# In-place softmax features, three KV banks, a centred second layernorm, and reciprocals as a power on GpSimd

## The chip, the cores and the metric

The kernel runs on one core of a Trainium2 chip. The metric is the device time of one execution in microseconds; the first result is the median of two executions of each kernel, an experiment's that of four or six, and e2 and e6 ran once, for the profile. This core has no second die to compare with, so an execution counts as slow when it lies over 1.5% above the fastest of its kernel. Engines are named as the profile names them: PE (TensorE, matmuls), PEld (its weight loads), DVE (VectorE), ACT (ScalarE), POOL (GpSimd) and SP (DMA issue).

## The reference, cut to what matters

```python
def _A_ref(x, wqkv, w_phi, wo):            # S = 2048, D = 640, H = 32 heads of Dh = 20
    q, k, v = ...                          # x @ wqkv
    pq = einsum("bhsd,hdf->bhsf", q, w_phi);  pk = einsum("bhsd,hdf->bhsf", k, w_phi)
    phi_q = concat([softmax(pq), softmax(-pq)], -1)      # 64 softmaxes of 20 for each row
    phi_k = concat([softmax(pk), softmax(-pk)], -1)
    kv = einsum("bhsf,bhsd->bhfd", phi_k, v);  z = phi_k summed over s
    o = einsum("bhqf,bhfd->bhqd", phi_q, kv) / (einsum("bhqf,bhf->bhq", phi_q, z)[..., None] + 1e-6)
    return o.reshape(B, S, D) @ wo
def _B_ref(x, w_gate, w_up, w_down):       # F = 1536
    return ((x @ w_gate) * (x @ w_up)) @ w_down
h  = x + _A_ref(layernorm(x), ...)
h2 = h + _B_ref(layernorm(h), ...)
```

The rows are handled in 16 tiles of 128. All k tiles must be done before `kv` exists, and all of `kv` before the first numerator `phi_q @ kv`. So there are three stages: features and KV accumulation; a transition (numerators, normaliser, output projection, second layernorm, first FFN matmul); then four blocks of FFN, with the remaining q tiles made beside them.

## The kernel before

The program is written through a recorder. It gets a list of operations with **declared costs**, finds an order for each engine by list scheduling with these costs, and inserts semaphore waits wherever two operations touch the same **64-byte granule** of SBUF. The parts that matter:

```python
GRAN = 64
def _keys(self, ap):                  # which granules an operand touches
    ...
        b0, b1 = o * esz, (o + span) * esz - 1
        for g in range(b0 // gran, b1 // gran + 1):
            keys.add((name, g))
# resolve(): a write of a key waits for that key's last writer and readers; a read for its writer
...
def program(name):                    # each engine runs its list in order
    ...
        for o in op.deps:
            eng.wait_ge(*o.val)
        ins = op.fn(eng)
...
    e_p  = pool("e", sb("e_r", 3 * 2 * D), 0, 2 * D, 3)          # three buffers of exponentials
    sr_p = pool("sr", sb("sr", 3 * 4 * H, FP32), 0, 4 * H, 3)    # 128 floats each: sums, reciprocals
...
    def soft(ps, outs):
        ek = e_p.new()
        sr = sr_p.new()
        act(ek[:, 0:D], ps, ACT.Exp)
        act(ek[:, D:2 * D], ps, ACT.Exp, scale=-1.0)
        R.add("vector", lambda e: e.tensor_reduce(...), [ek], [sr[:, 0:2 * H]], cost=1.48)
        R.add("vector", lambda e: e.reciprocal(out=real(sr)[:, 2 * H:4 * H], in_=real(sr)[:, 0:2 * H]), ..., cost=0.56)
        for dst, esel, rsel in outs:                              # 2 (k) or 3 (q) multiplies
            tt("gpsimd", dst, esel(ek), rsel(rr), ALU.mult)
...
    acc = psum.new(2, starts=(6,))             # KV chunks 0 to 7, beside the projections
    acc2 = psum.new(1, starts=(7, 6))          # chunks 8 to 10: a second pass after the features
...
    def watt(t):                               # output projection, residual, second layernorm
        ...
        tt("vector", x_all[:, t, :], pr[:, 0:D], x_all[:, t, :], ALU.add)
        ln_stats(t)                            # two batch statistics and their aggregate, DVE
        ln_rs(t, 1)                            # Ln, Exp on ACT, one small DVE operation
        ln_apply(t, hT[:, b, :, P * q:P * (q + 1)])
```

The softmax here doesn't subtract the row's maximum and nothing guards it: scores larger than these inputs give would overflow.

## Time and profile before

| | |
|---|---|
| median | 337.76 us (337.29 to 338.23) |
| profiled span | 331.5 us (another execution, of 333.26 us) |
| busy: PE, DVE, ACT, POOL | 295.8, 184.9, 154.0, 89.9 us |
| first numerator matmul | 97.2 us |
| first FFN matmul | 136.0 us |

The windows view gives the busy time of each engine in a stretch, with the granted PE clock (PEclk). From 140 us on, PE is busy 9.8 us or more in every 10 us at clock 1.00, but for the last 11 us. The stretch ahead of that is where time is to be had:

```profile
core 0: us, PE busy (x) PEld busy (x) DVE busy (x) ACT busy (x) POOL busy (x), PEclk, DMA share, GB/s
70.00:80.00 10.00, 6.55 (x58) 4.07 (x58) 5.19 (x6) 4.99 (x8) 5.18 (x6) 1.00 0.00 1
90.00:100.00 10.00, 6.61 (x57) 5.38 (x57) 6.55 (x16) 4.04 (x9) 7.88 (x9) 0.83 0.72 173
100.00:110.00 10.00, 7.48 (x26) 3.17 (x27) 2.67 (x4) 6.82 (x14) 2.64 (x3) 0.68 0.90 177
120.00:130.00 10.00, 5.20 (x22) 1.94 (x20) 8.04 (x20) 9.05 (x22) 4.97 (x6) 0.88 0.60 115
```

The groups by form for the softmax features. After the count stand busy us and the mean ns of one, then the engine's idle time before them and what ended it:

```profile
L717 DVE TENSOR_REDUCE sr<-e_r 128x64 f32<-128x1280 bf16 x32 | 46.4, 1464 | 16.7 <-ACT e_r L590 16.7
L596 POOL TENSOR_TENSOR phq<-e_r,sr 128x600 bf16<-128x600 bf16 x32 | 37.8, 1202 | 111.3 <-DVE sr L720 98.3 <-DMA wkv<-phq 6.9 <-DVE mv L672 5.4
L596 POOL TENSOR_TENSOR r<-e_r,sr 128x1200 bf16<-128x1200 bf16 x16 | 35.5, 2227 | 27.5 <-DVE sr L720 27.5
L720 DVE RECIPROCAL sr<-sr 128x64 f32<-128x64 f32 x32 | 16.8, 537 | 0.3
```

The waits view (who waited for whom: us in total, times, longest). ACT's exponentials wait for POOL, as an e buffer is free only after POOL's multiply. DVE's reduces wait for ACT:

```profile
DVE sr L717 <- ACT e_r L590: 16.7, 10, 6.6
ACT e_r L590 <- POOL phq L596: 8.4, 5, 3.0
ACT e_r L590 <- POOL r L596: 4.6, 3, 3.5
```

And two lines of the timeline, in which a small DVE operation with two SBUF inputs, 0.15 us where no POOL instruction runs beside it, lasts almost as long as the POOL multiply beside it:

```profile
36.93 2.22 POOL L596 TENSOR_TENSOR r<-e_r,sr 128x1200 bf16<-128x1200 bf16 x1 [3.13 <-DVE sr L720]
37.18 1.99 DVE L672 SCALAR_TENSOR_TENSOR mv<-mv 128x2 f32<-128x2 f32 x1
```

### The profile page before, as it was taken

Reading aid. Unit: us, or ns where it says so; the run is one execution under the profiler, and the core shown is the slowest. Engines: PE = TensorE matmul, PEld = TensorE weight load, DVE = VectorE, ACT = ScalarE, POOL = GpSimd, SP = SyncE. Lnnn points to the kernel's source line nnn. Section 1 sums busy time; section 2 is a strip of 40 time slices with the busy share of each in tenths; the row PEclk is TensorE's granted clock in tenths of the full one; section 3 lists DMA queues with packets and bytes.
Section 4 is the critical chain, followed back from the end, with each engine's and each line's share of the span. In section 5 each row is a group of like instructions: output and inputs, shape, how many; then the busy total and the mean of one; then the engine's idle time right before and its main releaser. Section 6 shows DMA issues by size and latency. Waiting matters only on the chain.

```text
span 331.5 us, 4759 instructions
## 1 busy us (share of the span) xinstructions
PE 295.8 (89%) x1856; PEld 155.2 (47%) x1890; DVE 184.9 (56%) x328; ACT 154.0 (46%) x287; POOL 89.9 (27%) x104
## 2 busy tenths in 40 slices
PE   2988899859576894999999999999999999999996
PEld 2646666436262331444455444445543445544453
DVE  3898998726963586736541346955234583133331
ACT  4787797724638558621520675331048342022200
POOL 7147678685782036230000002303000000000000
PEclk9999999999977896899999999999999999999999
DMA  8567098930579236140301000541300013100011
GB/s 243 158 164 213 5 208 203 244 129 2 103 177 220 44 63 128 21 88 0 61 20 59 22 0 0 65 83 42 104 0 2 2 21 77 42 0 2 0 42 59
DMA packets 55466, 25.82 MB, mean 78 GB/s; under 512 B 45935, under 2 KB 54163, under 8 KB 55443
## 3 DMA queue, kind: packets, MB, share of 16 engines
q1 hardware_dynamic: 53299, 22.89, 30.8%
q10 hardware_dynamic: 2144, 2.62, 2.4%
q8 instruction: 15, 0.25, 0.3%
q14 instruction: 8, 0.07, 0.1%
HBM read 11.87 MB, written 2.62 MB: 44 GB/s over the span
## 4 chain that ended last, share of the span: by engine, by line
PE 71%; DVE 10%; ACT 9%; POOL 5%; issue 2%; DMA 2%; SPq 0%; POOLq 0%; ACTq 0%
PE ps L579 70%; DVE sr L717 4%; ACT e_r L590 3%; POOL r L596 3%; ACT xn L677 2%; DMA r<-in_A_wqkv_dram 2%; DVE st L664 1%; DVE mv L672 1%; ACT r L590 1%; PE ps L691 1%; DVE sr L720 1%; DVE r L596 1%; ACT lnd L590 1%; POOL phq L596 1%; POOL r L614 1%
## 5 line engine op out<-in xcount | busy, mean ns | idle before, releaser
L579 PE MATMUL ps<-xnT,wgu 128*128 128x512 bf16 x469 | 105.7, 379 | 1.2 <-issue 0.5
L590 ACT ACTIVATE r<-ps 128x512 bf16<-128x512 f32 (+3 forms) x88 | 53.0, 611 | 93.7 <-PE ps L579 93.4
L596 DVE TENSOR_TENSOR r<-ps,r 128x512 bf16<-128x512 f32 (+2 forms) x72 | 49.0, 689 | 75.5 <-PE ps L579 49.2
L579 PE MATMUL ps<-r 128*128 128x128 bf16 (+6 forms) x612 | 71.4, 274 | 4.5 <-DVE KV L802 3.8
L596 POOL TENSOR_TENSOR phq<-e_r,sr 128x600 bf16<-128x600 bf16 (+1 forms) x48 | 42.2, 910 | 111.3 <-DVE sr L720 98.3
L579 PEld LDWEIGHTS ps<-xnT,wgu 128*128 128x128 bf16 x480 | 45.8, 98 | 56.6 <-issue 2.4
L579 PEld LDWEIGHTS ps<-r 128*128 128x128 bf16 (+2 forms) x620 | 46.7, 113 | 29.6 <-DVE KV L802 4.2
L717 DVE TENSOR_REDUCE sr<-e_r 128x64 f32<-128x1280 bf16 x32 | 46.4, 1464 | 16.7 <-ACT e_r L590 16.7
L579 PE MATMUL ps<-wkv,xnT 128*128 128x128 bf16 (+1 forms) x310 | 45.3, 297 | 8.3 <-ACT e_r L590 4.8
L590 ACT ACTIVATE e_r<-ps 128x640 bf16<-128x640 f32 x64 | 41.8, 703 | 19.6 <-POOL phq L596 8.4
L596 POOL TENSOR_TENSOR r<-e_r,sr 128x1200 bf16<-128x1200 bf16 (+1 forms) x32 | 40.1, 1274 | 27.9 <-DVE sr L720 27.5
L579 PEld LDWEIGHTS ps<-wkv,xnT 128*128 128x128 bf16 x320 | 24.2, 98 | 26.1 <-ACT e_r L590 5.6
L596 DVE TENSOR_TENSOR r<-ps,x_all 128x640 bf16<-128x640 f32 x16 | 13.1, 821 | 34.5 <-PE ps L579 34.5
L664 DVE BATCH_NORM_STATS2 st<-x_all 128x6 f32<-128x320 bf16 x64 | 29.2, 479 | 4.0 <-DMA x_all<-in_A_x_dram 3.6
L579 PE MATMUL ps<-wq,xnT 128*128 128x512 bf16 (+1 forms) x155 | 26.8, 327 | 4.1 <-ACT e_r L590 1.7
L579 PE MATMUL ps<-wo,r 126*128 126x512 bf16 x192 | 29.8, 300 | 0.0
L677 ACT ACTIVATE xn<-x_all,mv 128x640 bf16<-128x640 bf16 x24 | 21.9, 915 | 6.4 <-DVE mv L672 6.3
L579 PEld LDWEIGHTS ps<-wo,r 126*128 126x128 bf16 x192 | 13.9, 97 | 15.7 <-issue 6.1
L579 PEld LDWEIGHTS ps<-wq,xnT 128*128 128x128 bf16 x160 | 13.4, 107 | 15.8 <-issue 4.0
L590 ACT ACTIVATE lnd<-ps 6x512 f32<-6x512 f32 (+1 forms) x24 | 13.4, 578 | 13.9 <-PE ps L579 13.9
L720 DVE RECIPROCAL sr<-sr 128x64 f32<-128x64 f32 x32 | 16.8, 537 | 0.3
L596 DVE TENSOR_TENSOR x_all<-ps,x_all 128x640 bf16<-128x640 f32 x16 | 13.1, 820 | 5.6 <-PE ps L579 5.6
(40 smaller groups left out, 112.6 us busy)
## 6 DMA issues: line engine op xcount, KB each, us to landing
out_dram<-r SPq DMA_DIRECT2D x16, 160.0 KB, 1.8
x_all<-in_A_x_dram ACTq DMA_DIRECT2D x3, 640.0 KB, 5.0
wgu<-in_B_w_gate_dram SPq DMA_DIRECT2D x5, 384.0 KB, 4.8
wgu<-in_B_w_up_dram SPq DMA_DIRECT2D x5, 384.0 KB, 6.0
r<-in_B_w_down_dram SPq DMA_DIRECT2D x6, 320.0 KB, 5.2
r<-in_A_wqkv_dram SPq DMA_DIRECT2D x2, 800.0 KB, 5.2
wkv<-in_A_wqkv_dram SPq DMA_DIRECT2D x1, 800.0 KB, 10.0
wo<-in_A_wo_dram SPq DMA_DIRECT2D x4, 157.5 KB
```

The lines of the kernel that those rows point to most:

```text
L579: return R.add("tensor", lambda e: e.matmul(real(o), lhsT=real(l), rhs=real(r), start=start, stop=stop, **kw), [l, r], [o], cost=max(0.06, ...
L590: return e.activation(out=real(o), in_=real(i), func=func, scale=scale, **kw)
L596: return R.add(eng, lambda e: e.tensor_tensor(out=real(o), in0=real(a), in1=real(b), op=op), [a, b], [o], cost=cost)
L614: return R.add(eng, lambda e: e.memset(o, v), [], [o], cost=0.1 + numel(o) / 1100.0)
L664: R.add("vector", lambda e, k=k: e.bn_stats(st[:, t, 6 * k:6 * k + 6], x_all[:, t, 320 * k:320 * k + 320]), [x_all[:, t, 320 * k:320 * k + ...
L672: R.add("vector", lambda e: e.scalar_tensor_tensor(out=o, in0=m, scalar=-1.0, in1=r, op0=ALU.mult, op1=ALU.mult), [m, r], [o], cost=0.16)
L677: R.add("scalar", lambda e: e.activation(out=real(k), in_=x_all[:, t, :], func=ACT.Identity, bias=mv[:, t, 4:5], scale=mv[:, t, 3:4]), [x_ ...
L691: R.add("tensor", lambda e, o=o, i=i: e.transpose(out=real(o), in_=i, identity=ident[:, :]), [i, ident[:, :]], [o], cost=0.08, lat=0.17)
L717: R.add("vector", lambda e: e.tensor_reduce(out=real(sr)[:, 0:2 * H], in_=real(ek).rearrange("p (h f) -> p h f", f=DH), axis=AX.X, op=ALU. ...
L720: R.add("vector", lambda e: e.reciprocal(out=real(sr)[:, 2 * H:4 * H], in_=real(sr)[:, 0:2 * H]), [sr[:, 0:2 * H]], [sr[:, 2 * H:4 * H]], ...
```

## The change

The intent: exponentials are written straight to their final place and normalised there (no e buffers, one POOL multiply for each tile); the reciprocal leaves DVE; the third group of KV chunks is accumulated beside the features in a third bank; the second layernorm only subtracts the mean before the transpose, as the FFN is bilinear and its scale can be applied to the FFN's output. POOL also becomes an alternative place for both layernorm applications.

```diff
-    e_p = pool("e", sb("e_r", 3 * 2 * D), 0, 2 * D, 3)
-    phq_p = pool("phq", phq_r, 0, NCH * P, 2)
+    phq_p = pool("phq", phq_r, 0, NCH * P, NQ)          # NQ = 4
-    sr_p = pool("sr", sb("sr", 3 * 4 * H, FP32), 0, 4 * H, 3)
+    sr_p = pool("sr", sb("sr", 4 * 132, FP32), 0, 132, 4)
...                                                       # first layernorm's application
-              alts=[("vector", ..., 0.55)])
+              alts=[("vector", ..., 0.7),
+                    ("gpsimd", lambda e: e.tensor_scalar(...), 1.1)])
...
-        R.add("vector", lambda e: e.reciprocal(...), ..., cost=0.56)
+    def inverse(sr, n, o):
+        m1 = minus1[:, 0:1].to_broadcast([P, n])
+        R.add("gpsimd", lambda e: e.tensor_tensor(out=real(sr)[:, o:o + n], in0=real(sr)[:, 0:n], in1=m1, op=ALU.pow),
+              ..., cost=0.35)
+    def normalise(v, n):                                  # k tiles: n = 64, o = 66; q tiles: n = o = 66
+        sr = sr_p.new()
+        R.add("vector", lambda e: e.tensor_reduce(out=real(sr)[:, 0:n], in_=real(v), ...), ...)
+        inverse(sr, n, 66)
+        tt("gpsimd", v, v, sr[:, 66:66 + n].unsqueeze(2).to_broadcast([P, n, DH]), ALU.mult)
...
-    acc = psum.new(2, starts=(6,)); acc2 = psum.new(1, starts=(7, 6))
+    KV_BANKS = ((0, 1, 2, 3), (5, 6, 7, 8), (4, 9, 10))
+    accs = [psum.new(1, starts=(7,)), psum.new(1, starts=(6,)), psum.new(1, starts=(5,))]
...                                                       # watt(t)
-        tt("vector", x_all[:, t, :], ...); ln_stats(t); ln_rs(t, 1); ln_apply(t, hT[...])
+        h = h + pr, sum -> sm (DVE);  nm = -sm / D (DVE);  k = h + nm (ACT, or DVE 0.6, or POOL 1.1);  transpose k
+        k = k * k, sum -> ss (ACT);  r2 = exp(-ln(ss / D + eps)) (ACT)       # off the path
...                                                       # fd(t)
-        tt("vector", k, pr[:, 0:D], x_all[:, t, :], ALU.add)
+        k = pr * r2 + h (DVE)
```

More of the change, by code (lines that the diff above doesn't have):

```diff
@@ L2 @@
 from contextlib import ExitStack
-from concourse import mybir
+from concourse import bass, mybir
 FP32 = mybir.dt.float32
@@ L531, in _build @@
     hh_p = pool("hh", r1, NF * D, NF * 512, 2)
-    e_p = pool("e", sb("e_r", 3 * 2 * D), 0, 2 * D, 3)
-    phq_r = sb("phq", 2 * NCH * P)
-    phq_p = pool("phq", phq_r, 0, NCH * P, 2)
+    NQ = 4
+    phq_r = sb("phq", NQ * NCH * P)
+    phq_p = pool("phq", phq_r, 0, NCH * P, NQ)
     pqT_p = Pool("pqT", [sb("pqT", NCH * 512)[:, :], wkv_r[:, 0:NCH * 512]])
@@ L541, in _build @@
     mv = view(sb("mv", NT * 16, FP32), "p (t n) -> p t n", t=NT)
-    sr_p = pool("sr", sb("sr", 3 * 4 * H, FP32), 0, 4 * H, 3)
+    sr_p = pool("sr", sb("sr", 4 * 132, FP32), 0, 132, 4)
     Gm = view(sb("Gm", NC * H), "p (a h) -> p a h", a=NC)
     G6 = sb("G6", 32)
+    G6d = sb("G6d", 32)
     G10 = sb("G10", 32)
@@ L549, in _build @@
     epsb = sb("epsb", 16, FP32)
+    minus1 = sb("minus1", 16, FP32)
     PS = ctx.enter_context(nc.psum_tensor("ps", [P, 4096], FP32))
@@ L648, in _build @@
     memset("vector", epsb[:, :], EPS_LN)
+    memset("vector", minus1[:, :], -1.0)
     R.bias = 0.0
     memset("gpsimd", vaug[:, :, :].rearrange("p t (h e) -> p t h e", e=E21)[:, :, :, DH:E21], 1.0)
-    phq_clear = memset("gpsimd", phq_r[:, :].rearrange("p (k n) -> p k n", n=P)[:, :, 80:P], 0.0)
+    phq_clear = memset("gpsimd", phq_r[:, :].rearrange("p (k n) -> p k n", n=P)[:, :, 80:P], 1.0)
     memset("gpsimd", KV[:, 10, 0:HG], 0.0)
@@ L656, in _build @@
     afsel(G6[:, 0:HG], ALU.is_ge, 0.0, DH - 1, [[DH, HG]], -1)
-    tt("gpsimd", G10[:, 0:2], G6[:, 0:2], G6[:, 2:4], ALU.add)
+    memset("gpsimd", G6d[:, :], 1.0)
+    afsel(G6d[:, 0:HG], ALU.is_ge, 0.0, -100, [[DH, HG]], 1)
+    afsel(G6d[:, 0:HG], ALU.is_ge, 0.0, 119, [[-DH, HG]], -1)
+    tt("gpsimd", G10[:, 0:1], G6[:, 0:1], G6[:, 3:4], ALU.add)
+    tt("gpsimd", G10[:, 1:2], G6[:, 1:2], G6[:, 2:3], ALU.add)
     afsel(Em[:, :], ALU.is_ge, 0.0, -HG, [[1, P]], -DH)
@@ L680, in ln_apply @@
               alts=[("vector", lambda e: e.tensor_scalar(out=real(k), in0=x_all[:, t, :], scalar1=mv[:, t, 0:1],
-                                                         scalar2=mv[:, t, 3:4], op0=ALU.subtract, op1=ALU.mult), 0.55)])
+                                                         scalar2=mv[:, t, 3:4], op0=ALU.subtract, op1=ALU.mult), 0.7),
+                    ("gpsimd", lambda e: e.tensor_scalar(out=real(k), in0=x_all[:, t, :], scalar1=mv[:, t, 0:1],
+                                                         scalar2=mv[:, t, 3:4], op0=ALU.subtract, op1=ALU.mult), 1.1)])
         return dma(dst, k, 163840, tr=True)
@@ L709, in fold_M @@
         copy("any", dst, pr[:, 12:652])
-    def soft(ps, outs):
-        ek = e_p.new()
-        sr = sr_p.new()
-        act(ek[:, 0:D], ps, ACT.Exp)
-        act(ek[:, D:2 * D], ps, ACT.Exp, scale=-1.0)
-        R.add("vector", lambda e: e.tensor_reduce(out=real(sr)[:, 0:2 * H],
-                                                  in_=real(ek).rearrange("p (h f) -> p h f", f=DH),
-                                                  axis=AX.X, op=ALU.add), [ek], [sr[:, 0:2 * H]], cost=1.48)
-        R.add("vector", lambda e: e.reciprocal(out=real(sr)[:, 2 * H:4 * H], in_=real(sr)[:, 0:2 * H]),
-              [sr[:, 0:2 * H]], [sr[:, 2 * H:4 * H]], cost=0.56)
-        rr = sr[:, 2 * H:4 * H]
-        for dst, esel, rsel in outs:
-            tt("gpsimd", dst, esel(ek), rsel(rr), ALU.mult)
@@ L726, in tail_heads @@
-    def tail_heads(dst):
-        return (dst.rearrange("p (s h f) -> p s h f", s=2, f=DH),
-                lambda ek: ek.rearrange("p (s h f) -> p s h f", s=2, f=DH)[:, :, 30:32, :],
-                lambda r: r.rearrange("p (s h) -> p s h", s=2)[:, :, 30:32].unsqueeze(3).to_broadcast([P, 2, 2, DH]))
-    def outs_k(t):
-        d = phik[:, t, :]
-        return [
-            (d[:, 0:1200].rearrange("p (s h f) -> p s h f", s=2, f=DH),
-             lambda ek: ek.rearrange("p (s h f) -> p s h f", s=2, f=DH)[:, :, 0:30, :],
-             lambda r: r.rearrange("p (s h) -> p s h", s=2)[:, :, 0:30].unsqueeze(3).to_broadcast([P, 2, 30, DH])),
-            tail_heads(d[:, 1200:1280]),
-        ]
@@ L740, in outs_q @@
-    def outs_q(k):
-        k = k.rearrange("p (c n) -> p c n", c=NCH)
-        res = []
-        for s in range(2):
-            res.append((k[:, NG * s:NG * (s + 1), 0:120].rearrange("p c (h f) -> p c h f", f=DH),
-                        lambda ek, s=s: ek[:, D * s:D * s + 600].rearrange("p (c h f) -> p c h f", c=NG, f=DH),
-                        lambda r, s=s: r[:, H * s:H * s + 30].rearrange("p (c h) -> p c h", c=NG).unsqueeze(3)
-                        .to_broadcast([P, NG, HG, DH])))
-        res.append(tail_heads(k[:, 10, 0:80]))
-        return res
+    def inverse(sr, n, o):
+        m1 = minus1[:, 0:1].to_broadcast([P, n])
+        R.add("gpsimd", lambda e: e.tensor_tensor(out=real(sr)[:, o:o + n], in0=real(sr)[:, 0:n], in1=m1, op=ALU.pow),
+              [sr[:, 0:n], minus1[:, 0:1]], [sr[:, o:o + n]], cost=0.35)
@@ new lines, in normalise, with heads_down @@
+    def normalise(v, n):
+        sr = sr_p.new()
+        R.add("vector", lambda e: e.tensor_reduce(out=real(sr)[:, 0:n], in_=real(v), axis=AX.X, op=ALU.add),
+              [v], [sr[:, 0:n]], cost=0.13 + n * DH / 960.0)
+        inverse(sr, n, 66)
+        tt("gpsimd", v, v, sr[:, 66:66 + n].unsqueeze(2).to_broadcast([P, n, DH]), ALU.mult)
+    def heads_down(ap):
+        v = ap.rearrange("p (h f) -> p h f", f=DH)
+        part, (s, n), inner = v.ap
+        return bass.AP(v.tensor, v.offset + s * (n - 1), [list(part), [-s, n], list(inner)])
@@ new lines, in soft_k, with soft_q, down, fn @@
+    def soft_k(t, ps):
+        act(phik[:, t, 0:D], ps, ACT.Exp)
+        act(heads_down(phik[:, t, D:2 * D]), ps.rearrange("p (h f) -> p h f", f=DH), ACT.Exp, scale=-1.0)
+        normalise(phik[:, t, :].rearrange("p (h f) -> p h f", f=DH), 2 * H)
+    def soft_q(ps, k):
+        k3 = k.rearrange("p (c n) -> p c n", c=NCH)
+        act(k3[:, 0:NG, 0:120], ps[:, 0:600].rearrange("p (c n) -> p c n", c=NG), ACT.Exp)
+        act(k3[:, 10, 0:40], ps[:, 600:D], ACT.Exp)
+        def down(o, dims):
+            def fn(s):
+                v = k.fn(s)
+                return bass.AP(v.tensor, v.offset + o, [list(v.ap[0])] + dims)
+            return Lazy(k.buf, fn)
+        act(down(NG * P + 100, [[P, NG], [-DH, HG], [1, DH]]),
+            ps[:, 0:600].rearrange("p (c h f) -> p c h f", c=NG, f=DH), ACT.Exp, scale=-1.0)
+        act(down(10 * P + 60, [[-DH, 2], [1, DH]]), ps[:, 600:D].rearrange("p (h f) -> p h f", f=DH), ACT.Exp, scale=-1.0)
+        k4 = k3[:, :, 0:120].rearrange("p c (h f) -> p c h f", f=DH)
+        n = NCH * HG
+        sr = sr_p.new()
+        def r4(o):
+            return sr[:, o:o + n].rearrange("p (c h) -> p c h", c=NCH)
+        R.add("vector", lambda e: e.tensor_reduce(out=real(r4(0)), in_=real(k4), axis=AX.X, op=ALU.add),
+              [k4], [r4(0)], cost=0.13 + n * DH / 960.0)
+        inverse(sr, n, n)
+        tt("gpsimd", k4, k4, r4(n).unsqueeze(3).to_broadcast([P, NCH, HG, DH]), ALU.mult)
@@ L772, in k_proj @@
         mark.setdefault("kv_proj", []).append(u)
-        soft(pr[:, 0:D], outs_k(t))
+        soft_k(t, pr[:, 0:D])
         return u
@@ L777, in chunk_heads @@
         return (HG * (c % NG), HG, 120) if c < 2 * NG else (30, 2, 80)
-    acc = psum.new(2, starts=(6,))
-    acc2 = psum.new(1, starts=(7, 6))
+    KV_BANKS = ((0, 1, 2, 3), (5, 6, 7, 8), (4, 9, 10))
+    accs = [psum.new(1, starts=(7,)), psum.new(1, starts=(6,)), psum.new(1, starts=(5,))]
     def kv_place(c):
-        return (acc, 512 * (c // 4) + 126 * (c % 4)) if c < 8 else (acc2, 126 * (c - 8))
-    def kv_acc(t, chunks):
+        for k, cs in enumerate(KV_BANKS):
+            if c in cs:
+                return accs[k], 126 * cs.index(c), cs[0] == c
@@ L786, in kv_acc, with k_rows @@
+    def k_rows(t, c):
+        if c < NG:
+            return phik[:, t, 120 * c:120 * c + 120]
+        if c < 2 * NG:
+            o = 2 * D - 120 * (c - NG + 1)
+            return phik[:, t, o:o + 120]
+        return phik[:, t, 600:680]
+    def kv_acc(t, k):
         with R.group() as u:
             mark.setdefault("kv_acc", []).append(u)
-            for c in chunks:
+            for c in KV_BANKS[k]:
                 h0, nh, kr = chunk_heads(c)
-                a, c0 = kv_place(c)
-                mm(a[0:kr, c0:c0 + E21 * nh], phik[:, t, 120 * c:120 * c + kr],
-                   vaug[:, t, E21 * h0:E21 * (h0 + nh)], c % 4 == 0 and t == 0, t == NT - 1, skip=True)
@@ L794, in kv_evac @@
-    def kv_evac(c):
-        h0, nh, kr = chunk_heads(c)
-        a, c0 = kv_place(c)
-        g = (G6 if c < 2 * NG else G10)[0:kr, 0:nh]
-        psv = a[0:kr, c0:c0 + E21 * nh].rearrange("p (h e) -> p h e", e=E21)
-        tt("vector", KV[0:kr, c, HG:HG + DH * nh].rearrange("p (h d) -> p h d", d=DH), psv[:, :, 0:DH],
-           g.unsqueeze(2).to_broadcast([kr, nh, DH]), ALU.mult)
-        o, i = KV[0:kr, c, 0:nh], psv[:, :, DH]
+                a, c0, first = kv_place(c)
+                mm(a[0:kr, c0:c0 + E21 * nh], k_rows(t, c),
+                   vaug[:, t, E21 * h0:E21 * (h0 + nh)], first and t == 0, t == NT - 1, skip=True)
@@ new lines, in kv_acc, with kv_evac @@
+        return u
+    def kv_evac(c, n):
+        h0, nh, kr = chunk_heads(c)
+        a, c0, _ = kv_place(c)
+        g = (G6 if c < NG else G6d if c < 2 * NG else G10)[0:kr, 0:nh].unsqueeze(1).to_broadcast([kr, n, nh])
+        psv = a[0:kr, c0:c0 + E21 * nh * n].rearrange("p (c h e) -> p c h e", c=n, e=E21)
+        tt("vector", KV[0:kr, c:c + n, HG:HG + DH * nh].rearrange("p c (h d) -> p c h d", d=DH), psv[:, :, :, 0:DH],
+           g.unsqueeze(3).to_broadcast([kr, n, nh, DH]), ALU.mult)
+        o, i = KV[0:kr, c:c + n, 0:nh], psv[:, :, :, DH]
@@ L824, in q_proj @@
         k = phq_p.new()
-        soft(pr[:, 0:D], outs_q(k))
+        soft_q(pr[:, 0:D], k)
         dma(pqT[b].rearrange("p (c n) -> p c n", c=NCH)[:, :, P * tt_:P * (tt_ + 1)], k, NCH * 32768, tr=True)
@@ L849, in num @@
         mm(pr[0:m, 512:1024], Em[0:nh, 0:m], rden[0:nh, :], True, True)
-        act(rx[0:m, :], pr[0:m, 512:1024], ACT.Copy)
+        i, o = pr[0:m, 512:1024], rx[0:m, :]
+        R.add("scalar", lambda e: e.activation(out=real(o), in_=real(i), func=ACT.Copy), [i], [o], cost=0.6, lat=0.08,
+              alts=[("vector", lambda e: e.tensor_copy(real(o), real(i)), 0.67)])
         tt("vector", oT[b][0:m, 512 * c:512 * (c + 1)], pr[0:m, 0:512], rx[0:m, :], ALU.mult)
@@ L860, in watt @@
                     mm(pr[:, n0:n1], oT[b][0:m, 512 * c + P * q:512 * c + P * (q + 1)], Wo6[0:m, c, n0:n1], c == 0, c == 5)
-        tt("vector", x_all[:, t, :], pr[:, 0:D], x_all[:, t, :], ALU.add)
-        ln_stats(t)
-        ln_rs(t, 1)
-        ln_apply(t, hT[:, b, :, P * q:P * (q + 1)])
+        h, sm, nm, ss, r2 = (x_all[:, t, :], *(mv[:, t, k:k + 1] for k in (8, 9, 10, 11)))
+        R.add("vector", lambda e: e.scalar_tensor_tensor(out=h, in0=real(pr)[:, 0:D], scalar=1.0, in1=h, op0=ALU.mult,
+                                                         op1=ALU.add, accum_out=sm), [pr[:, 0:D], h], [h, sm], cost=0.85)
+        ts("vector", nm, sm, -1.0 / D, ALU.mult)
+        k = xn_p.new()
+        R.add("scalar", lambda e: e.activation(out=real(k), in_=h, func=ACT.Identity, bias=nm), [h, nm], [k], cost=0.8,
+              lat=0.08, alts=[("vector", lambda e: e.tensor_scalar(out=real(k), in0=h, scalar1=nm, scalar2=None, op0=ALU.add), 0.6),
+                              ("gpsimd", lambda e: e.tensor_scalar(out=real(k), in0=h, scalar1=nm, scalar2=None, op0=ALU.add), 1.1)])
+        dma(hT[:, b, :, P * q:P * (q + 1)], k, 163840, tr=True)
+        R.add("scalar", lambda e: e.activation(out=real(k), in_=real(k), func=ACT.Square, accum_out=ss), [k], [k, ss],
+              cost=0.9, lat=0.08)
+        act(r2, ss, ACT.Ln, bias=epsb[:, 0:1], scale=1.0 / D)
+        act(r2, r2, ACT.Exp, scale=-1.0)
     hh = {}
@@ L889, in fd @@
         k = ot_p.new()
-        tt("vector", k, pr[:, 0:D], x_all[:, t, :], ALU.add)
+        h, r2 = x_all[:, t, :], mv[:, t, 11:12]
+        R.add("vector", lambda e: e.scalar_tensor_tensor(out=real(k), in0=real(pr)[:, 0:D], scalar=r2, in1=h, op0=ALU.mult,
+                                                         op1=ALU.add), [pr[:, 0:D], r2, h], [k], cost=0.82)
         dma(out[0, P * t:P * (t + 1), :], k, 163840, writes=[])
     tr_u, kv_u = [], []
+    MINI = 11
     def ln_group(t0, n):
@@ L910, in _build @@
     for t in range(NT):
-        kv_u.append((v_proj(t), k_proj(t)))
-        kv_acc(t, range(8))
+        kv_u.append([v_proj(t), k_proj(t)])
+        for k in range(2):
+            kv_acc(t, k)
+        if t == MINI:
+            for m in range(t + 1):
+                u = kv_acc(m, 2)
+                R.after(kv_u[t], u)
+        elif t > MINI:
+            kv_acc(t, 2)
         if t % 2 == 0 and t < 12:
@@ L936, in _build @@
             bulk(6 + 2 * c + g, Wgu[:, g, c, :], (B_w_gate, B_w_up)[g][P * c:P * (c + 1), :], 393216)
-    for c in range(8):
-        kv_evac(c)
+    kv_evac(0, 4)
+    kv_evac(5, 4)
+    for c in (4, 9, 10):
+        kv_evac(c, 1)
     for t in range(4):
         q_proj(t)
-    for t in range(NT):
-        kv_acc(t, range(8, 11))
-    for c in range(8, 11):
-        kv_evac(c)
     for f in range(0, NF, 2):
```

## The prediction

> **What bounds the kernel now.** The engine table gives PE 89% busy, but the 10 us windows split the span in two. From 131 us on, PE is busy 9.8 to 9.95 us of every 10 at clock 1.00: matmul-bound, and the change removes no matmuls. Before that, PE idles about 30 us: 70 to 130 us has 42.1 us of PE busy in 60, and the granted clock drops to 0.68 to 0.88 in three windows there.
>
> There, where the gain must come from, the chain of waits runs through the softmax features: one POOL stretch of 6.87 us at 66 us, then ACT exponentials, VectorE reduces (2.88 us) and reciprocals (0.87 us), a second KV pass of 48 small matmuls (about 4.9 us at 93 us), then logarithm, exponential and layernorm. The waits view shows ACT exponentials held 8.4 + 4.6 us by POOL: only three e buffers, freed when POOL has multiplied.
>
> **What changes, per tile.**
> - VectorE loses the reciprocal: 0.537 us x 32 = 16.8 us in all, about 11 us of it before the FFN.
> - POOL: k goes from 2.227 + 0.321 us to one multiply of 1280 elements, about 2.36 us by the trace's slope; q from 2 x 1.20 + 0.33 to one of 1320, about 2.43 us. It gains a power on 64 to 66 float32 elements. No trace shows that cost. An 80-element multiply takes 0.32 us; a power should take more. Estimate 0.3 to 1.0, point 0.6 us.
> - The e buffers go. Exponentials land in their final place, so ACT and PE can run ahead of POOL; phq goes from 2 to 4 buffers.
> - q exponentials are 4 instructions instead of 2: about 0.4 us more ACT per q tile.
> - The third KV bank removes the 4.9 us second pass and most of the 22 small evacuations (about 4.3 us of VectorE), but late projections have two PSUM pairs instead of three.
> - Second layernorm: per tile VectorE drops 2 x 0.48 + 0.20 + 0.21 us, and ACT's Ln and Exp (0.48 us) leave the path to the transpose: about 1.7 us shorter latency, four tiles in the critical transition. ACT gains a Square of about 0.9 us, off the path.
>
> **On the critical path.** POOL must process 20 tiles before the first numerator: 20 x (2.4 + 0.6) = 60 us from about 21 us, so to about 84 us with some idle, near PE's own floor; the projection and accumulation now end at 97. I credit 9 us there, 7 us for the transition (evacuation, layernorm, fewer cold-clock stretches), none for the FFN, minus 1 us for PSUM pressure. Sum: about 15 us.
>
> The Trainium skill, GPSIMD Engine Reference, section 1 Specifications, says POOL's SBUF interfaces are shared with VectorE when the latter reads two SBUF inputs. The trace agrees: a scalar-tensor-tensor of 128x2 took 1.99 us while a POOL multiply ran, against 0.15 otherwise.
>
> **Prediction: 322.5 us, 80% range 309 to 338.** Faster by over 2%: 0.70; within 2%: 0.18; slower: 0.12.
>
> **Right if:** the first steady FFN window starts near 116 us instead of 131; no burst of 48 KV matmuls stands after the last feature; no waits of ACT exponentials on POOL; POOL over 85% busy from 30 to 80 us; power near 0.6 us.
>
> **Wrong if:** the power is over about 1.2 us: then 20 tiles of POOL run past 97 us and eat the gain (at 2 us the kernel is slower); or VectorE stalls behind POOL; or two PSUM pairs hold PE.

## The result, and the profile after

| | before | after |
|---|---|---|
| median | 337.76 us | 632.6 us (632.16 to 633.04) |
| profiled span | 331.5 us | 630.4 us |
| POOL busy | 89.9 us | 448.3 us |
| granted clock, mean | 0.974 | 0.751 |
| first numerator / first FFN matmul | 97.2 / 136.0 us | 306.5 / 404.9 us |

The ratio of after to before is 1.8696 (95% interval 1.8485 to 1.8906). Ratios here are the mean time of one kernel's fast runs over that of the other's of the same rounds, so they are not quite the ratio of the medians quoted. The kernel before moved between 335.65 and 339.42 us (median) from one group of runs to the next; compare ratios across groups.

The page's part on the chain that ended last, before (first fence) and after (second fence). PE's 71% became POOL's 67%:

```profile
PE 71%; DVE 10%; ACT 9%; POOL 5%; issue 2%; DMA 2%; SPq 0%; POOLq 0%; ACTq 0%
```

```profile
POOL 67%; PE 25%; DVE 3%; DMA 3%; issue 1%; ACT 1%; SPq 0%; POOLq 0%; DVEq 0%
```

POOL's groups by form after. L723 is the power:

```profile
L723 POOL TENSOR_TENSOR sr<-sr,minus 128x66 f32<-128x66 f32 x16 | 174.4, 10899 | 60.5 <-DVE sr L763 60.5
L723 POOL TENSOR_TENSOR sr<-sr,minus 128x64 f32<-128x64 f32 x16 | 168.5, 10532 | 6.4 <-DVE sr L728 6.1
L598 POOL TENSOR_TENSOR phq<-phq,sr 128x1320 bf16<-128x1320 bf16 x16 | 38.7, 2422 | 0.9
L598 POOL TENSOR_TENSOR r<-r,sr 128x1280 bf16<-128x1280 bf16 x16 | 37.6, 2355 | 3.5 <-DVE sr L728 3.2
L689 POOL TENSOR_SCALAR xn<-x_all,mv 128x640 bf16<-128x640 bf16 x7 | 17.5, 2501 | 2.6 <-DMA xnT<-xn 1.6 <-DVE mv L679 1.0
```

A power takes 10.5 to 10.9 us where 0.6 was predicted and 0.35 was declared. The two multiplies are as predicted (2.36 and 2.42 us). A layernorm application on POOL takes 2.50 us where 1.1 was declared.

The windows view after, three stretches in which POOL is all but alone:

```profile
40.00:60.00 20.00, 0.00 (x0) 0.00 (x0) 0.00 (x0) 0.00 (x0) 20.00 (x3) 0.50 0.08 16
260.00:280.00 20.00, 0.00 (x0) 0.00 (x0) 1.53 (x1) 1.43 (x4) 20.00 (x3) 0.50 0.21 57
320.00:340.00 20.00, 0.00 (x0) 0.00 (x0) 1.53 (x1) 0.00 (x0) 18.14 (x4) 0.50 0.29 84
```

The waits view after, in answer to the one before. The reduces (L728 for k, L763 for q) now wait for **POOL**, though a tile's reduce needs only that tile's exponentials and a free one of the four buffers of sums:

```profile
DVE sr L728 <- POOL sr L723: 90.0, 3, 34.2
DVE sr L763 <- POOL phq L598: 84.0, 5, 38.8
DVE sr L763 <- POOL sr L723: 67.2, 3, 45.6
DVE sr L728 <- POOL r L598: 52.9, 3, 25.4
```

The timeline after shows one such wait end: a reduce starts only as the power is over.

```profile
49.75 10.54 POOL L723 TENSOR_TENSOR sr<-sr,minus 128x64 f32<-128x64 f32 x1
60.26 2.35 POOL L598 TENSOR_TENSOR r<-r,sr 128x1280 bf16<-128x1280 bf16 x1
60.32 1.49 DVE L728 TENSOR_REDUCE sr<-r 128x64 f32<-128x1280 bf16 x1 [23.42 <-POOL sr L723]
```

### The profile page after: what moved, and what is told of

It is laid out like the page before. It is cut to its first block, busy times and chain, and to the rows that moved or that the text cites. A ratio compares the mean times of both kernels' runs of the same rounds, so it can differ in the third digit from the quotient of the medians.

```text
span 630.4 us, 4766 instructions
## 1 busy us (share of the span) xinstructions
PE 330.5 (52%) x1890; PEld 167.9 (27%) x1890; DVE 163.3 (26%) x268; ACT 155.6 (25%) x327; POOL 448.3 (71%) x101
## 4 chain that ended last, share of the span: by engine, by line
POOL 67%; PE 25%; DVE 3%; DMA 3%; issue 1%; ACT 1%; SPq 0%; POOLq 0%; DVEq 0%
POOL sr L723 53%; PE ps L581 25%; POOL r L598 6%; POOL phq L598 6%; POOL xn L689 2%; DMA xnT<-xn 2%; DVE sr L763 1%; DVE sr L728 1%; DMA r<-in_A_wqkv_dram 1%; POOL xn L899 1%; ACT r L592 0%; SPq L575 0%; DVE r L931 0%; ACT xn L901 0%; ACT phq L592 0%
## 5 line engine op out<-in xcount | busy, mean ns | idle before, releaser
L723 POOL TENSOR_TENSOR sr<-sr,minus 128x64 f32<-128x64 f32 (+1 forms) x32 | 342.9, 10715 | 66.9 <-DVE sr L763 60.5
L581 PE MATMUL ps<-r 128*128 128x512 bf16 (+5 forms) x620 | 78.4, 289 | 158.2 <-POOL r L598 141.6
L592 ACT ACTIVATE r<-ps 128x640 bf16<-128x640 f32 (+1 forms) x96 | 60.6, 646 | 97.8 <-PE ps L581 97.5
L581 PE MATMUL ps<-wkv,xnT 128*128 128x512 bf16 x320 | 55.4, 337 | 47.5 <-ACT phq L592 32.4
L763 DVE TENSOR_REDUCE sr<-phq 128x66 f32<-128x1320 bf16 x16 | 24.2, 1526 | 159.8 <-POOL phq L598 84.0
L728 DVE TENSOR_REDUCE sr<-r 128x64 f32<-128x1280 bf16 x16 | 23.2, 1475 | 145.1 <-POOL sr L723 90.0
L592 ACT ACTIVATE phq<-ps 128x600 bf16<-128x600 f32 (+1 forms) x64 | 23.4, 441 | 119.6 <-DMA pqT<-phq 108.8
L598 POOL TENSOR_TENSOR r<-r,sr 128x1280 bf16<-128x1280 bf16 x16 | 37.6, 2355 | 3.5 <-DVE sr L728 3.2
L598 POOL TENSOR_TENSOR phq<-phq,sr 128x1320 bf16<-128x1320 bf16 x16 | 38.7, 2422 | 0.9
L901 ACT ACTIVATE xn<-xn 128x640 bf16<-128x640 bf16 x16 | 11.7, 729 | 33.1 <-DMA xnT<-xn 33.1
L689 POOL TENSOR_SCALAR xn<-x_all,mv 128x640 bf16<-128x640 bf16 x7 | 17.5, 2501 | 2.6 <-DMA xnT<-xn 1.6
```

The source lines that it names most:

```text
L581: return R.add("tensor", lambda e: e.matmul(real(o), lhsT=real(l), rhs=real(r), start=start, stop=stop, **kw), [l, r], [o], cost=max(0.06, ...
L592: return e.activation(out=real(o), in_=real(i), func=func, scale=scale, **kw)
L598: return R.add(eng, lambda e: e.tensor_tensor(out=real(o), in0=real(a), in1=real(b), op=op), [a, b], [o], cost=cost)
L689: ("gpsimd", lambda e: e.tensor_scalar(out=real(k), in0=x_all[:, t, :], scalar1=mv[:, t, 0:1], scalar2=mv[:, t, 3:4], op0=ALU.subtract, op ...
L723: R.add("gpsimd", lambda e: e.tensor_tensor(out=real(sr)[:, o:o + n], in0=real(sr)[:, 0:n], in1=m1, op=ALU.pow), [sr[:, 0:n], minus1[:, 0: ...
L728: R.add("vector", lambda e: e.tensor_reduce(out=real(sr)[:, 0:n], in_=real(v), axis=AX.X, op=ALU.add), [v], [sr[:, 0:n]], cost=0.13 + n * ...
```

## The experiments

Theory A: the power, 10.7 us each, is the whole loss. Theory B: the order found from a wrong declared cost is a large part of it. Theory C: another part of the change also costs much. Eighteen kernels ran. A number in parentheses is the ratio to the kernel before in the same rounds, with its 95% interval.

### e1: all of the change, the reciprocals on VectorE

```diff
-        R.add("gpsimd", lambda e: e.tensor_tensor(..., in1=m1, op=ALU.pow), ..., cost=0.35)
+        R.add("vector", lambda e: e.reciprocal(out=real(sr)[:, o:o + n], in_=real(sr)[:, 0:n]), ..., cost=0.56)
```

> All of the change, but the 32 reciprocals back on VectorE. Theory A (the power on GpSimd, 10.7 us each, is the whole loss): the rest of the change gains what I predicted for it or more, 312 to 326 us. Theory C (another part, such as only two PSUM pairs or busier GpSimd, also costs much): over 345 us. The reciprocal itself should measure about 0.54 us again.

331.72 us (0.9864, 0.9806 to 0.9922). With the power gone the loss is gone, but the rest gains only 1.4%: outside A's range, and far from C's. This opened the second question: where are my predicted 15 us?

### e2: the power as the only edit of the kernel before

```diff
-        R.add("vector", lambda e: e.reciprocal(...), ..., cost=0.56)
+        R.add("gpsimd", lambda e: e.tensor_tensor(..., in1=m1, op=ALU.pow), ..., cost=0.35)
```

> The kernel before with the power on GpSimd as its only edit. Theory A: 32 x (10.7 + 2.6) us = 426 us of GpSimd work, of which 24 tiles (319 us) stand before or within the transition, so 580 to 680 us, with the power again near 10.7 us. If the power is slow only in the company of the rest (its broadcast operand's place, in-place buffers, VectorE contention): under 420 us and a power well under 5 us.

603.71 us, one look, state unknown. The power took 10.53 us here too, for k and for q tiles. In-place buffers and the rest of the change are not needed to make it slow. Its buffers of sums are still the old 128 floats, and no reduce waits for POOL in its waits view; this matters at the end.

### e3: the power with its true cost declared

```diff
-              ..., cost=0.35)
+              ..., cost=10.7)
```

> The changed kernel, with the scheduler told 10.7 us for a power in place of 0.35. Theory B (the order made from a wrong cost is a large part of the loss): under 520 us. Theory A (GpSimd's throughput): 20 tiles x 13.1 us = 262 us before the first numerator plus about 22 us of start, then 4 more in the transition, then about 220 us for the rest: 530 to 620 us, so at most 15% better than the 632.6 us.

538.78 us (1.5999, 1.5917 to 1.6082). The time lies in the range of A. A better order recovers 94 us of the 295 lost, so the wrong cost is a real part of it, but throughput remains: POOL is busy 429.3 us.

### e4: a multiply of the same shape in the power's place

```diff
-              ... op=ALU.pow)          # times minus1 = -1.0
+              ... op=ALU.mult)         # times 1/400, as the sums are near 20
```

> The changed kernel with one operation name exchanged: multiply by 1/400 in place of power -1, same operands, shapes and engine. It is close to the reciprocal only because the sums are near 20, so it is a probe of the time and a wrong kernel in principle. Theory A: the instruction falls from 10.7 to about 0.3 us and the kernel to 308 to 322 us, a little under e1. If shape, float32 operands or the broadcast operand were the cost, the instruction stays at several us.

337.06 us (1.0007, 0.9933 to 1.0081). The declared cost stayed 0.35, so every engine has the same order as in the changed kernel. The instruction fell from 10.7 us to 0.30 us:

```profile
L723 POOL TENSOR_TENSOR sr<-sr,minus 128x64 f32<-128x64 f32 (+1 forms) x32 | 9.6, 299 | 91.0 <-DVE sr L763 84.7
```

So the operation itself is dear, not its shape, its float32 operands or its broadcast operand, and 632.6 - 337.1 = 295.5 us of time go with it. That is 89% of the 32 x (10.71 - 0.30) = 333 us that it adds to POOL. But the whole kernel missed the expected 308 to 322 us: **even an almost free power gains nothing over the kernel before**, as the rest of the change stood (e19 comes back to this).

### e6: the power on half of each k tile's sums

As e8 below, with 32 of the 64 k sums by the power and the rest by the reciprocal.

> As e8, with the first 32 of the 64 sums of each k tile raised to the power on GpSimd and all others by the reciprocal on VectorE. If the cost goes with the elements, the power of 32 takes 5.2 to 5.5 us; if it is a fixed cost of the call, about 10.5 us. The kernel: 16 x (5.4 + 2.36) + 4 x 2.42 = 134 us of GpSimd before the first numerator, from about 20 us on, plus 200 to 220 us: 365 to 395 us.

```profile
L722 POOL TENSOR_TENSOR sr<-sr,minus 128x32 f32<-128x32 f32 x16 | 86.4, 5419 | 7.5 <-DVE mv L679 7.5
```

402.67 us (one look), a little over my range. From 32 to 64 elements the power grows by 5.1 us: about 160 ns for each element of a partition and 0.3 us fixed. Between 32 and 66 elements it scales with their number, so by this line (an estimate) one call for several tiles would save only the fixed 0.3 us of each.

### e8: e1 without GpSimd for the layernorms

```diff
-                    ("gpsimd", lambda e: e.tensor_scalar(out=real(k), in0=x_all[:, t, :], ...), 1.1)])
-                              ("gpsimd", lambda e: e.tensor_scalar(out=real(k), in0=h, ...), 1.1)])
```

> The changed kernel with the reciprocals on VectorE (as e1) and without GpSimd as a place for the two layernorm applications. In e1 GpSimd took 14 of them at 1.88 to 2.50 us, 32.4 us, where the scheduler had been told 1.1 us. Theory D (these misplaced layernorms ate what the rest of the change gains): 312 to 324 us, GpSimd busy about 85 us in all, no layernorm on GpSimd in the chain. Theory E (the rest of the change is worth little by itself, as the projections were not bound by what it removes): 328 to 334 us, as e1.

328.95 us (0.9787, 0.9747 to 0.9826). In e1 POOL had taken 14 layernorms at more than their declared cost:

```profile
L689 POOL TENSOR_SCALAR xn<-x_all,mv 128x640 bf16<-128x640 bf16 x10 | 24.9, 2498 | 8.0 <-DVE mv L679 7.7 <-DMA xnT<-xn 0.3
L898 POOL TENSOR_SCALAR xn<-x_all,mv 128x640 bf16<-128x640 bf16 x4 | 7.5, 1883 | 60.4 <-DVE mv L603 60.4
```

Without them the ratio is 0.8 points better, which is hardly more than what an accident of order did (0.7, e13 below), so that the layernorms cost time is not shown. By the median the result lies at the better end of E's range; most of the missing gain is still missing.

### e9, e14: the cheap operation on GpSimd, without the layernorms there

e9 is e8 with e4's multiply; e14 is e9 with another declared cost (0.30 for 0.35), as a control of the order.

> As e8, but the reciprocal replaced by the multiply by 1/400 on GpSimd (a probe of time, a wrong kernel in principle): what a power at 0.3 us would have given at best. Theory D: 310 to 324 us, within 4 us of e8, as GpSimd gains 9.6 us and VectorE loses 17 us. Theory E: 328 to 337 us. If GpSimd is what binds the features, e9 is slower than e8 in spite of the lighter VectorE.

> Control: e9 (multiply in place of the power) with the scheduler told 0.30 us, which is what it measures, in place of 0.35. If e9's 335 us was an accident of order: 326 to 331 us, so that a cheap power would have matched the reciprocal on VectorE. If GpSimd binds: 333 to 337 us again.

334.97 us (0.9938, 0.9896 to 0.9980) and 335.37 us (0.9963, 0.9916 to 1.0009). Two orders agree: with the cheap operation on POOL the first numerator comes at 99.0 and 98.5 us, with the reciprocal on DVE (e8) at 90.2. I took this to mean that POOL's load binds. That reading fell with e19.

### e10: the reciprocal as Ln and Exp on ACT

```diff
+        act(sr[:, o:o + n], sr[:, 0:n], ACT.Ln)
+        act(sr[:, o:o + n], sr[:, o:o + n], ACT.Exp, scale=-1.0)
```

> As e8, with the reciprocal as a logarithm and an exponential on ACT (two small activations of 0.25 to 0.3 us by the durations of similar small ones), so neither VectorE nor GpSimd has it. Against e8: VectorE loses 17 us of work, ACT gains 16 to 18 us. If VectorE binds the features, 3 to 6 us faster than e8; if GpSimd or PE does, within 2 us of e8; if ACT does, slower.

334.99 us over all runs, two of four slow; the two fast runs are 334.44 and 329.86 us (0.9874, 0.9798 to 0.9950). Inconclusive against e8.

### e11, e12, e13: what each part is worth, and a control

e11 puts the old second layernorm back into e8. e12 puts two KV banks and the second pass back. e13 changes only the declared cost of the reciprocal (0.50 for 0.56), so the order alone.

> As e8 (change without power and without layernorms on GpSimd, 328.95 us), with the second layernorm as before (batch statistics, Ln and Exp ahead of the application). My sum gave the transition about 5 us of gain from the centred form. If that holds: 332 to 336 us, and the first matmul of the FFN about 4 to 6 us later than e8's 127.6 us. If the transition is bound by the numerators' normaliser (Ln, Exp, broadcast matmul, copy, multiply) and not by the layernorm: 327 to 331 us.

> As e8, with two KV banks and the second pass over chunks 4, 9 and 10 after the features, as before. If the third bank is what moved the first numerator from 97.2 to 90.2 us: it goes back to 94 to 98 us and the kernel to 332 to 337 us. If the earlier end comes from the in-place buffers: 327 to 331 us and the first numerator near 90 to 92 us.

> Control: e8 with the same instructions, but the scheduler told 0.50 us for a reciprocal in place of 0.56, so only their order differs. It shows how far an accident of order moves the time: within 2 us of e8 means that the 2 to 6 us differences between my variants are effects of the edits; 4 us or more means that they cannot be told from luck of the schedule.

| kernel | median us | ratio | first numerator, first FFN matmul (us) |
|---|---|---|---|
| e8 | 328.95 | 0.9787 | 90.2, 127.6 |
| e11, old layernorm | 330.74 | 0.9829 (0.9790 to 0.9869) | 88.6, 127.6 |
| e12, two banks (one of six runs slow) | 332.43 | 0.9859 (0.9812 to 0.9905) | 93.4, 130.3 |
| e13, other order | 327.56 | 0.9719 (0.9676 to 0.9763) | 89.4, 126.9 |

The control moves the time by 0.7%, as much as the third bank (0.7%) and more than the centred layernorm (0.4%). These two cannot be told from luck of the order, and no more can the layernorms on POOL (e1 against e8, 0.8 points). Two banks put the first numerator 3.2 us later than in e8, a little under half of what e8 had gained there. My 5 us for the centred layernorm are not there: the first FFN matmul came at 127.6 us with either, and from the first numerator to it the old form took 39.0 us and the centred one 37.4.

### e15: no normaliser

```diff
-        act(lnd, pr, ACT.Ln); act(rden, lnd, ACT.Exp, scale=-1.0); mm(pr[0:m, 512:1024], Em, rden); copy; tt(..., ALU.mult)
+        R.add("vector", lambda e: e.tensor_copy(real(o), real(i)), [i], [o], cost=0.67)
```

> A wrong kernel on purpose: e8 with the numerators copied out unnormalised, so without Ln, Exp, broadcast matmul, copy and multiply between a numerator and the output projection (24 times). If that chain binds the transition, the time from the first numerator to the first FFN matmul falls from e8's 37.4 us to 28 us or less, and the kernel to 315 to 321 us. If the transition is bound by the softmax of the next q tiles or by the clock alone: 35 us or more, and 325 us or more.

323.13 us (0.9660, 0.9607 to 0.9714), with a wrong output. From first numerator (98.0) to first FFN matmul (137.9) took 39.9 us, not 28 or less. The kernel's time falls between the two ranges expected. The test turned out less clean than I meant it. The scheduler found another order: the first numerator came 7.8 us later than in e8, and the profile has 170 matmuls between it and the first FFN matmul, against 133 in e8, so the 39.9 us are not for the same work. From the first numerator to the end e15 takes 224.4 us and e8 236.1. Of these 11.7 us, the PE time of the 24 broadcast matmuls left out is about 5 (24 x 0.22 us, an estimate by the 30 matmuls of this width that e16 ran back to back in 6.64 us); the rest is not accounted for. PE's idle time between the two marks did not fall (9.9 us against 6.6 in e8), so no sign is seen that the chain of logarithm, exponential, broadcast and copy binds the transition; that it does not is not shown.

### e7: the power where POOL is otherwise idle

As e8, with the power for q tiles 8 to 15 alone and 10.9 us declared.

> e8, with the power on GpSimd for the q tiles 8 to 15 alone, which are made beside the FFN while GpSimd is otherwise idle, and the scheduler told 10.9 us. Each group of four takes 4 x 13.3 = 53 us of GpSimd, and one block of FFN lasts about 54 us in e8. If the loss is only where GpSimd is on the chain: 328 to 336 us, so at most 2% over e8, for 8 powers that cost 87 us of GpSimd.

343.14 us (1.0239, 1.0173 to 1.0305): the powers cost 4.5 points over e8, more than expected, though POOL idles through most of the FFN in e8. But the loss is not beside the FFN: from the first FFN matmul to the end e7 takes 196.0 us and e8 198.7 (1040 and 1072 matmuls), and PE idles 6.0 and 4.6 us of that. It stands ahead of it, as the first FFN matmul comes at 146.3 us (127.6 in e8) and three of the eight powers start before that. A piece of the chain shows how one of them delays the path to the FFN:

```profile
110.66 10.92 POOL sr L722
121.67 1.53 DVE sr L765
124.05 1.74 PE ps L581 x3
```

A VectorE *reduce* (L765) starts only when the *power* of another tile ends, after 8.2 us of idle DVE. The residual addition stands behind it in DVE's list, and PE sits idle 8.2 us for that. Why should a reduce wait for another tile's power?

### e16, e17: a warm PE clock through the transition

Sums over 5 us slices (5 us times one minus the granted clock, PE's idle time included) give the clock a cost of at most 8.6 us between 85 and 140 us, in the kernel before and in e8 alike. I had credited "fewer cold-clock stretches". The Trainium skill, "TensorE: Matmul & The Clock Gate" (Part 1), says that the clock falls to half after an idle window of about 3.4 us; the traces agree in part. In the kernel before PE was busy 0.42 us of the 3 us from 126 us on, and the clock was 0.50 in the next 3; but a gap of 3.40 us before 74.80 us was followed by 1.00. These two kernels fill PE's gaps with 40 pairs of dummy matmuls at the lowest priority (e16 in e8's program, e17 in e13's).

```diff
+    for i in range(40):
+        with R.group() as u:                       # R.bias = -1e5: only where PE has nothing else
+            for _ in range(2):
+                mm(pd[:, 0:512], ident[:, :], x_all[:, 0:1, 0:512]..., True, True)
+        R.after(kv_u[12][1], u)
```

> e8 with 40 pairs of dummy matmuls (17 us of full-rate work, results unused) at the lowest priority after the features, so that the scheduler drops them into TensorE's idle gaps of the transition. In both the kernel before and e8 the granted clock between 85 and 140 us costs 8.6 us (5 us slices, one minus the clock, summed). If that cold clock is what keeps the transition from shrinking: the clock there rises to 0.95 or more and the kernel falls to 320 to 326 us in spite of the added work. If the waits alone bind: no gain, 329 to 334 us.

> The same 40 pairs of dummy matmuls in e13 (327.56 us), as a second order of the same work. Cold clock as the cause: 319 to 325 us. Waits alone: 327 to 333 us.

331.26 us (0.9895, 0.9823 to 0.9967) and 335.38 us (1.0011, 0.9933 to 1.0090). (In these rounds six of eleven runs of the kernel before count as slow, so the ratios are to its quicker runs.) The windows of e16 show the clock at full rate:

```profile
90.00:100.00 10.00, 9.95 (x55) 4.81 (x54) 6.34 (x16) 2.88 (x10) 9.61 (x4) 1.00 0.64 99
100.00:110.00 10.00, 9.94 (x42) 4.20 (x42) 6.86 (x9) 7.23 (x14) 4.85 (x2) 1.00 0.52 98
110.00:120.00 10.00, 9.32 (x49) 3.98 (x48) 6.11 (x9) 6.39 (x15) 0.00 (x0) 1.00 0.11 20
```

It did not help: e16 is within the range for waits alone, and e17 is slower than both ranges and 7.8 us over e13. The dummies also moved the first numerator to 100.1 us, so this does not show that the clock is harmless; it shows that keeping it warm in this way pays nothing.

### e18, e19: padded buffers of sums

In the kernel before a buffer of sums is 128 floats, 512 bytes, exactly 8 granules of 64 bytes. The change made it 132 floats: 8.25 granules. So a tile's last reciprocals (from float 128 on in the first buffer, from 124 and 120 on in the next two) share a granule with the first sums of the next buffer. The recorder sees a conflict and makes the reduce of a later tile wait until POOL has read the reciprocals of the tile in the neighbouring buffer. The scheduler, which treats the buffers as separate, knows nothing of it.

```diff
-    sr_p = pool("sr", sb("sr", 4 * 132, FP32), 0, 132, 4)
+    sr_p = pool("sr", sb("sr", 4 * 144, FP32), 0, 144, 4)
```

This takes the conflict away, not a needed wait: with 144 floats (9 granules) no two buffers meet in a granule. Every engine has the same instructions in the same order as in e13 (for e18) and e14 (for e19). Only waits differ. The program has, of the waits of a reduce for POOL, 9 of 18 for the neighbouring buffer in e13 and 14 of 20 in e14, and none in e18 and e19; the others are for the earlier use of its own buffer.

> e13 (327.56 us; all of the change but the power and the layernorms on GpSimd), with each buffer of the softmax sums padded from 132 to 144 floats and nothing else; every engine has the same instructions in the same order. The recorder tracks SBUF in 64-byte granules, and 132 floats are 8.25 of them, so neighbouring tiles' sums share a granule and a VectorE reduce waits for GpSimd's multiply of the tile before (4.1 + 2.6 us of such waits in e13, 8.3 + 2.9 in e8, none in the kernel before). If these waits bind the features: no VectorE reduce waits for GpSimd, the first numerator comes 2 to 6 us sooner than e13's 89.4 us, and the kernel takes 321 to 326 us. If they only fill slack: 326 to 329 us.

> The same padding in e14 (335.37 us; multiply of the power's shape on GpSimd), where VectorE reduces waited 22.5 us for GpSimd. If the shared granules are why even a 0.3 us operation on GpSimd loses to the reciprocal on VectorE: 322 to 329 us and the first numerator near 90 us (e14: 98.5). If GpSimd's load is: 332 to 336 us.

| kernel | median us | ratio | first numerator, first FFN matmul (us) |
|---|---|---|---|
| e13 | 327.56 | 0.9719 | 89.4, 126.9 |
| e18 = e13 padded | 320.41 | 0.9468 (0.9409 to 0.9528) | 84.3, 120.7 |
| e14 | 335.37 | 0.9963 | 98.5, 137.9 |
| e19 = e14 padded (two of six runs slow) | 321.77 | 0.9477 (0.9380 to 0.9574) | 88.1, 124.7 |

Both theories of shared granules held (both times ended just under the ranges given), and e18 beats both kernels: it is the best correct one found, 5.3% faster than the kernel before. The waits of the reduces in e13:

```profile
DVE sr L760 <- ACT phq L592: 9.0, 4, 3.1
DVE sr L725 <- POOL r L598: 4.1, 3, 2.5
DVE sr L725 <- ACT r L592: 3.1, 3, 1.7
DVE sr L760 <- POOL phq L598: 2.6, 2, 1.4
```

and in e18, where POOL is gone from them:

```profile
DVE sr L760 <- ACT phq L592: 9.8, 4, 3.9
DVE sr L725 <- ACT r L592: 2.7, 3, 1.2
```

The timeline at the same place of the order. In e13 a reduce begins as POOL's multiply of another tile ends:

```profile
52.32 2.36 POOL L598 TENSOR_TENSOR r<-r,sr 128x1280 bf16<-128x1280 bf16 x1 [4.53 <-DVE sr L720]
54.71 1.49 DVE L725 TENSOR_REDUCE sr<-r 128x64 f32<-128x1280 bf16 x1 [2.47 <-POOL r L598]
```

In e18 it runs beside that multiply:

```profile
50.07 1.43 DVE L725 TENSOR_REDUCE sr<-r 128x64 f32<-128x1280 bf16 x1
50.23 2.36 POOL L598 TENSOR_TENSOR r<-r,sr 128x1280 bf16<-128x1280 bf16 x1 [3.75 <-DVE sr L720]
```

The waits of e14's reduces for POOL, none of which is left in e19:

```profile
DVE sr L761 <- POOL phq L598: 13.1, 5, 7.9
DVE sr L761 <- POOL sr L721: 5.3, 2, 2.8
DVE sr L726 <- POOL r L598: 3.7, 2, 2.9
DVE sr L726 <- POOL sr L721: 0.4, 1, 0.4
```

The waits seen add up to 6.7 us in e13 and 22.5 us in e14; padding gained 7.2 and 13.6 us by the medians, which are from different rounds, and 2.5 and 4.9 points of the ratio. In e18 the features have little more to give, as PE is busy 48.3 of the 50 us from 30 to 80 us. In e14 a tile needs DVE, then POOL twice, then DVE for the next tile: with the shared granule these cannot overlap.

## Why the prediction was wrong

**The step that failed: "Estimate 0.3 to 1.0, point 0.6 us" for the power on POOL.** It measured 10.5 us for 64 elements and 10.9 for 66. The prediction named the danger ("if the power is over about 1.2 us ... at 2 us the kernel is slower") but gave slower a chance of only 0.12. I had argued from a multiply of 80 elements (0.32 us) and the code declared 0.35 us. The Trainium skill, "GPSIMD Engine Reference" (section 3.1), gives about 2.6 cycles an element for two-input arithmetic; the multiply of 1280 elements agrees roughly (2.36 us, which at the page's 1.2 GHz is 2.2 cycles). No page gives a power. Put the measured 10.7 us into my own sum and it says 20 x (2.4 + 10.7) = 262 us of POOL before the first numerator in place of 60, from about 21 us on; the trace has the first numerator at 306.5 us. Exchanging this one operation (e4) gives back 295.5 us.

The other points:

- *"Most gain ahead of the FFN"*: right. After the first FFN matmul, the kernel before takes 331.5 - 136.0 = 195.5 us and e18 319.1 - 120.7 = 198.4 us.
- *"I credit 9 us" for the features, minus 1 for PSUM*: the first numerator came 7.0 us earlier in e8 and 12.9 us earlier in e18 (97.2 to 84.3). The mechanism, that ACT and PE run ahead of POOL, was right: ACT's exponentials waited 13.0 us for POOL before and do not wait for it in e18. The shared granule held it back.
- *"7 us for the transition"*: from first numerator to first FFN matmul it was 38.8 us before, 37.4 in e8, 36.4 in e18. The gain is 1.4 to 2.4 us. The cold clock stayed (8.6 us in e8 as before), and the centred layernorm did not move the first FFN matmul (e11). What binds this stretch I did not find: e15 gives no sign that it is the normaliser but does not rule it out, and a warm clock bought with dummies does not pay (e16, e17).
- *"None for the FFN"*: right, by 195.5 us before and 198.4 in e18. The powers of the late q tiles (e7) cost their time ahead of the FFN, 8.2 us of it in one reduce that waits for the neighbouring buffer. e7 was not run with padded buffers, so how much of its 14 us they explain stays open.
- *Not seen at all*: POOL as a place for layernorms at a declared 1.1 us that takes 1.9 to 2.5 (0.8 points of the ratio, e1 against e8, not told from luck of the order), and the 132-float buffers (2.5 points of the ratio between e13 and e18, nearly 5 between e14 and e19). Both stood in the diff.

The sum of 15 us, "322.5 us", is about what the change gives once the power, the layernorms on POOL and the buffers are mended: 320.4 us with the reciprocal on DVE, 321.8 us with a cheap operation on POOL. As a ratio 0.955 was predicted, and 0.947 and 0.948 measured. It reached that value with a larger gain in the features than I had put down and a smaller one in the transition, so the agreement is partly luck. Moving the reciprocal off DVE is not seen to be worth anything here, even at 0.3 us: e18 and e19 do not differ beyond their intervals.

Open: how much of 632.6 us padding alone would give back. The reduces waited 294 us for POOL in the waits shown above, but not all of that is false: of the program's 18 such waits 4 are for the reduce's own buffer, and POOL was busy in 448 of 630 us. e2, with the power and without a shared granule, still took 603.71 us. Padding with the power in place was not run.

## What to carry to other kernels

A cost of an operation that no trace shows is the first thing to measure; until then, give it a range of orders of magnitude, whatever the code declares. When a scheduler places work by declared costs, check every alternative that it is offered against a measured duration. When the waits view shows an engine waiting for one that it needs nothing from, look for storage that the two share at the granularity of the dependency tracking: here twelve floats of padding were worth more (2.5 and 4.9 points) than the third KV bank and the centred layernorm together (1.1 points in e11 and e12).

## What the Trainium skill lacked or had wrong

- "GPSIMD Engine Reference" has no cost for a power. Measured: 5.42 us for 32, 10.53 us for 64 and 10.90 us for 66 float32 elements of each partition, about 160 ns an element, against 0.29 us for a multiply of 64 in the same place.
- "GPSIMD Engine Reference", section 4.1 (Engine selection), calls one-input elementwise operations on GpSimd roughly line-rate. A tensor-scalar of 640 bf16 elements took 2.50 us with two per-partition scalars and 1.88 us with one: 3.9 and 2.9 ns an element. The kernel before has the same two-scalar operation on VectorE eight times: 0.39 to 0.45 us six times, and 1.29 and 1.90 us in the two that ran beside a POOL instruction.
- "SBUF — State Buffer", section "SBUF: two separate sides", says that the port pair shared by GpSimd and a VectorE instruction with two SBUF inputs is an exclusive lock held for the whole instruction. The trace agrees: 1.99 us for a 128x2 operation beside a 2.22 us multiply, 0.15 us with no POOL instruction beside it. The page needs no mending here, but a reader can take this look-alike for the lock: a one-input reduce that waits for a GpSimd multiply. That was a semaphore, not the lock: in e18 the same reduce (1.43 us) runs beside the same multiply (2.36 us).
- "TensorE: Matmul & The Clock Gate" (Part 1) gives "no PE-idle gaps" of over about 3.4 us as the rule. It does not say whether dummy matmuls are worth filling them with. Here they held the clock at 1.00 in e16 and gained nothing (331.26 us against e8's 328.95; e17 335.38 against e13's 327.56).
